# Attention, SoLU block and routed experts on one core: scatters declared independent, a fourth buffer for low parts, and both halves of a product in one slot

## Chip, cores and metric

The kernel runs on one core of one Trainium2 chip. The metric is the device time of one execution in microseconds, lower is better. Matmul operands are `float32r`: each value is kept as a high part and a low part, and a product is three matmuls (high by high, high by low, low by high).

## What is computed

Three layers in a row, over 8 batches of 3072 rows (24576 rows of 256 values):

```python
scores = (1/S) * z @ z.T                       # z: 8 x 3072 x 64
x = u * (relu(scores)**2 @ v)                  # attention, 256 columns
h = x @ w_in; sm = softmax(h); solu = h * sm   # 1024 columns
x = layernorm(solu) * g_ln @ w_out             # back to 256
logits = x @ w_gate; e = argmax(logits)        # 8 experts
out[row] = gate * (relu(x @ w1[e]) @ w2[e])    # w1: 256x1024, w2: 1024x256
```

## The kernel before

**Slots.** The whole program is one list of slots, written out by hand. Slot `n` of the attention is one block of 128 keys against a chunk of 512 queries: 8 batches of 6 chunks of 24 blocks are `NS` = 1152 slots. In a slot TensorE makes the scores `s` of a block four slots ahead (2 matmuls; blocks that were kept from the transposed pair are read back from memory instead) and adds the block at hand to the output, `pe_av`: 6 matmuls `o` of 128x512. ScalarE makes `r` (relu), `a` (square) and the high part `ah`; VectorE subtracts to get the low part `al` (`dve_lo`, line 463). `al` has three buffers, and in slot `n` it is made for block `n+2`.

**The block after the attention.** Each chunk's result is gated, split (`split_x`, line 492) and then worked on in the slots of the next chunk, four groups of 128 rows, one group every six slots: `blk_h` (line 503) is the first product, 12 matmuls `h`, of which the half `kd=0` is issued in slot `w` and the half `kd=1` in slot `w+1`; then maximum, exponent, a transposition over memory (`pb`, `moved`, `pT`), the split `pth`/`ptl`, and `blk_y` (line 577), 24 matmuls `yp` in two halves in two neighbouring slots. `blk_scale`, `blk_logits` and `blk_route` then compute the expert and the place of each row, with many small steps that go back and forth between GpSimd and VectorE (`vv`, `yi`, `rs`, `lg`, `gm`, `gk`, `gs`, `oh`, `ps`, `pf`, `pi`). `blk_scatter` (line 684) writes the 128 rows of a group to their places in `sorted_rows` in memory, by an indirect transfer that GpSimd issues.

**The experts.** `NU` = 62 units follow, 41 of 512 rows and 21 of 256, each with one expert's weights. A table of the first 37 (`n_early`) is made when chunks up to the fifth from the end have been counted, so that the units can start while the last chunks are still being routed; the table of the rest is made at the end. A unit has 8 steps. A step is `up` (6 matmuls `g`, relu on ScalarE, line 899, low part on VectorE, line 900) and, two steps later, `down` (12 matmuls `y`). The product `g` has two banks. After a unit's last `down`, each half of `y` is copied and its rows are written to their places in `out_y` by two indirect transfers from GpSimd (line 931), issued right there in the program.

**Loads.** For units from the third on, the rows `x` (8 pieces and the row numbers `gi`, `load_x`, line 830) and the weights (`load_w`, line 845, 1 MB each for `w1` and `w2`) are issued by SyncE, in order: rows 14 steps before the unit, `w1` of unit `i+2` in step 3 of unit `i` and `w2` in step 6. The split of those weights (`split_w`, lines 854 and 855) stands in steps 0 to 2 and 2 to 5 of unit `i+1`. Once the counts are final, `pad_tail` (line 771) writes 256 rows of padding behind each expert's rows, one expert every two steps from slot `NS+92` on, in SyncE's queue too: one transfer of 128x2x264.

**What waits.** The framework orders all transfers that touch the same tensor in memory by its own analysis: a scatter into `sorted_rows` or `out_y` waits until the one before has landed, a load of rows from `sorted_rows` waits for the scatters issued before it, a scatter for the loads before it, and a piece of padding for the piece before it.

Of the kernel before, what the change touches and what calls it, by code (L numbers as in the profile page):

```python
# [10 lines left out]
F32 = mybir.dt.float32  # L11
# [22 lines left out]
def attention_moe_kernel(ctx, tc, u, v, z, w_in, w_out, g_ln, w_gate, w1, w2, out):  # L34
# [56 lines left out]
    pad_row = const.tile([P, RW], F32, name="pad_row")  # L91
# [4 lines left out]
    index = const.tile([1, n_most], F32, name="index")  # L96

# [12 lines left out]
    with tc.manual_schedule():  # L110
# [14 lines left out]
        V.memset(pad_row[:, D:D + 1], PAD_ID)  # L125
# [3 lines left out]
    with ExitStack() as st:  # L129
# [111 lines left out]

        def fill_dummy():
            for h in range(HALF // P):
                nc.sync.dma_start(out=xs[DUMMY + h * P:DUMMY + (h + 1) * P], in_=pad_row)
# [255 lines left out]
        h_t, p_t, pt_t, y_t, st_t = {}, {}, {}, {}, {}  # L500
        pb_t, pT_t = {}, {}
# [133 lines left out]
        def blk_route(c, part):  # L635
# [23 lines left out]
            elif part == 5:  # L659
# [5 lines left out]
                G.tensor_tensor(out=counts, in0=cum[:, 3], in1=oh[:, 3], op=ALU.add)  # L665
                V.reciprocal(out=s["gs"], in_=s["gs"])
# [28 lines left out]
        def unit_table(parts, tail):  # L695
# [20 lines left out]
            for lo, n, size in parts:  # L716
# [5 lines left out]
                if size == HALF:  # L722
# [14 lines left out]
                ge = tb.tile([1, NE, n_most], F32, tag="ge", name="ge")[:, :, :n]  # L737
                it = index[:, :n]
                V.tensor_scalar(out=rw_f, in0=it, scalar1=float(size), scalar2=first, op0=ALU.mult, op1=ALU.add)
                yield  # L740
                V.tensor_tensor(out=ge, in0=it.unsqueeze(1).to_broadcast([1, NE, n]),
                                in1=pre.unsqueeze(2).to_broadcast([1, NE, n]), op=ALU.is_ge)
                yield
                V.tensor_reduce(out=ex_f, in_=ge.rearrange("o e n -> o n e"), axis=AX.X, op=ALU.add)
                yield
                V.tensor_tensor(out=ge, in0=ge, in1=step.unsqueeze(2).to_broadcast([1, NE, n]), op=ALU.mult)
                yield
                V.tensor_reduce(out=more_f, in_=ge.rearrange("o e n -> o n e"), axis=AX.X, op=ALU.add)
                V.tensor_tensor(out=rw_f, in0=rw_f, in1=more_f, op=ALU.add)
                yield  # L750
# [13 lines left out]
        table = {}  # L764

        def table_step(key, *args):
            if key not in table:
                table[key] = unit_table(*args)
            next(table[key], None)
# [21 lines left out]
        def take(name):  # L791
# [20 lines left out]
            elif name == "set1":  # L812
# [7 lines left out]
                c += [own(ap, "al", [P, CH], bufs=3) for _ in range(3)]  # L820
# [9 lines left out]
        def load_x(i, part=None):  # L830
# [10 lines left out]
            todo.append((gi_t[i][:, :n // P], unit[:, D:D + 1].rearrange("(q p) w -> p (q w)", p=P)))  # L841
            for dst, x in todo if part is None else todo[3 * part:3 * part + 3]:
                dma_of(i).dma_start(out=dst, in_=x)
# [66 lines left out]
        def down(k):  # L910
# [11 lines left out]
            for h, y in enumerate(y_p.pop(i)):  # L922
# [6 lines left out]
                for r in range(2):  # L929
                    q = 2 * h + r  # L930
                    G.indirect_dma_start(
                        out=out, out_offset=bass.IndirectOffsetOnAxis(ap=id_t[i][:, q:q + 1].bitcast(U32), axis=0),
# [209 lines left out]
```

## Time and profile before

| | us |
|---|---|
| median of three runs | 4299.98 |
| lowest and highest | 4298.31, 4304.7 |
| the profiled execution, its own time | 4297.59 |
| its span, first to last instruction | 4296.0 |
| TensorE busy in the span | 4218.8 (98%) |
| VectorE, ScalarE, GpSimd busy | 3173.4, 2773.7, 1368.9 |
| granted TensorE clock, mean | 0.994 of full |

A line of groups gives an operation's line, its shape and count, its busy time with the mean of one in ns, and the idle time just before it with what ended it. A line of waits gives who waited for whom, the total, how often and the longest. Matmuls overlap: one of 128x512 is drawn about 0.39 us long, and the next begins about 0.23 us after it, so the distance of two starts tells the pace, and a busy share of 100% does not tell that the pace is the best one.

### The profile page before, as it was taken

Reading aid. Unit: us, or ns where it says so; the run is one execution under the profiler, and the core shown is the slowest. Engines: PE = TensorE matmul, PEld = TensorE weight load, DVE = VectorE, ACT = ScalarE, POOL = GpSimd, SP = SyncE. Lnnn points to the kernel's source line nnn. Section 1 sums busy time; section 2 is a strip of 40 time slices with the busy share of each in tenths; the row PEclk is TensorE's granted clock in tenths of the full one; section 3 lists DMA queues with packets and bytes.
Section 4 is the critical chain, followed back from the end, with each engine's and each line's share of the span. In section 5 each row is a group of like instructions: output and inputs, shape, how many; then the busy total and the mean of one; then the engine's idle time right before and its main releaser. Section 6 shows DMA issues by size and latency. Waiting matters only on the chain.

```text
span 4296.0 us, 74103 instructions
## 1 busy us (share of the span) xinstructions
PE 4218.8 (98%) x23314; PEld 3659.4 (85%) x23314; DVE 3173.4 (74%) x5485; ACT 2773.7 (65%) x5104; POOL 1368.9 (32%) x2852
## 2 busy tenths in 40 slices
PE   7999999999999999999999999999889999999998
PEld 5888888888888888888888888888788899999998
DVE  8778787777878777787877778777655555555686
ACT  7767776776777677667767766775544444444565
POOL 5135224323522432352244235224322111111111
PEclk9999999999999999999999999999999999999999
DMA  6898789789888988997898898789655555555585
GB/s 160 168 173 180 171 181 176 165 183 174 179 170 182 175 166 183 173 177 171 182 174 168 183 174 176 169 169 181 143 143 132 147 147 134 145 137 147 156 221 162
DMA packets 2444332, 719.11 MB, mean 167 GB/s; under 512 B 2251933, under 2 KB 2325917, under 8 KB 2443936
## 3 DMA queue, kind: packets, MB, share of 16 engines
q1 hardware_dynamic: 2402016, 603.29, 69.2%
q0 software_dynamic: 40864, 110.95, 8.7%
q8 instruction: 182, 2.98, 0.3%
q14 instruction: 214, 1.75, 0.1%
q10 hardware_dynamic: 1056, 0.13, 0.0%
HBM read 442.35 MB, written 273.49 MB: 167 GB/s over the span
## 4 chain that ended last, share of the span: by engine, by line
PE 81%; issue 5%; DMA 4%; DVE 2%; SPq 2%; POOL 1%; ACT 1%; POOLq 0%; DVEq 0%; ACTq 0%
PE o L105 11%; PE o L106 11%; PE o L107 11%; PE yp L105 4%; PE yp L107 4%; PE yp L106 4%; PE h L512 4%; PE h L513 4%; PE h L516 4%; PE s L444 3%; PE s L445 3%; PE y L107 3%; PE y L106 3%; PE y L105 3%; PE g L105 3%
## 5 line engine op out<-in xcount | busy, mean ns | idle before, releaser
L106 PE MATMUL o<-al,vw 128*128 128x512 f32 x2304 | 908.2, 394 | 7.8 <-DVE al L465 7.3
L105 PE MATMUL o<-ah,vw 128*128 128x512 f32 x2304 | 907.8, 394 | 1.7 <-DVE ut L489 1.7
L107 PE MATMUL o<-ah,vw 128*128 128x512 f32 x2304 | 898.7, 390 | 0.0
L450 ACT ACTIVATE r<-s 128x512 f32<-128x512 f32 x704 | 416.7, 592 | 405.6 <-PE s L445 397.1
L460 ACT ACTIVATE ah<-a 128x512 fp32r<-128x512 f32 x832 | 525.3, 631 | 201.6 <-issue 99.5
L465 DVE TENSOR_TENSOR al<-a,ah 128x512 fp32r<-128x512 f32 x832 | 581.4, 699 | 15.7 <-ACT ah L460 14.7
L107 PEld LDWEIGHTS o<-ah,vw 128*128 128x128 f32 x2304 | 433.7, 188 | 94.4
L106 PEld LDWEIGHTS o<-al,vw 128*128 128x128 f32 x2304 | 433.6, 188 | 94.2 <-DVE al L465 16.3
L105 PEld LDWEIGHTS o<-ah,vw 128*128 128x128 f32 x2304 | 433.6, 188 | 84.9 <-ACT ah L460 2.1
L455 ACT ACTIVATE a<-r 128x512 f32<-128x512 f32 x704 | 438.0, 622 | 58.2 <-DVE al L465 29.5
L899 ACT ACTIVATE zw_x<-g 128x512 fp32r<-128x512 f32 (+1 forms) x332 | 179.9, 542 | 428.9 <-PE g L107 425.2
L107 PE MATMUL yp<-gw,ptl 128*128 128x264 f32 x1536 | 437.8, 285 | 7.0 <-DVE ptl L102 7.0
L105 PE MATMUL yp<-gw,pth 128*128 128x264 f32 x1536 | 438.8, 286 | 1.1 <-ACT pth L101 1.1
L106 PE MATMUL yp<-gw,pth 128*128 128x264 f32 x1536 | 438.0, 285 | 0.0
L900 DVE SCALAR_TENSOR_TENSOR zw_x<-g,zw_x 128x512 fp32r<-128x512 f32 (+1 forms) x332 | 205.6, 619 | 308.8 <-ACT zw_x L899 308.7
L102 DVE TENSOR_TENSOR ptl<-pT,pth 128x512 fp32r<-128x512 f32 x384 | 264.2, 688 | 215.8 <-ACT pth L101 213.7
L686 POOL DMA_INDIRECT sorted_rows<-y,pi x192 | 211.7, 1102 | 390.3 <-DMA sorted_rows<-y,pi 307.9
L513 PE MATMUL h<-w_in,xt 128*128 128x512 f32 x768 | 304.9, 397 | 0.0
L512 PE MATMUL h<-w_in,xt 128*128 128x512 f32 x768 | 304.6, 397 | 0.0
L105 PEld LDWEIGHTS yp<-gw,pth 128*128 128x128 f32 x1536 | 289.2, 188 | 16.9 <-ACT pth L101 1.5
L106 PEld LDWEIGHTS yp<-gw,pth 128*128 128x128 f32 x1536 | 289.9, 189 | 15.0
L107 PEld LDWEIGHTS yp<-gw,ptl 128*128 128x128 f32 x1536 | 290.1, 189 | 7.7 <-DVE ptl L102 7.7
(271 smaller groups left out, 10665.7 us busy)
## 6 DMA issues: line engine op xcount, KB each, us to landing
vw_x<-in_moe_w SPq DMA_DIRECT2D x120, 1024.0 KB
pT<-moved SPq DMA_DIRECT2D x768, 128.0 KB
sym<-kept SPq DMA_DIRECT2D x1520, 64.0 KB
kept<-sym SPq DMA_DIRECT2D x316, 256.0 KB
moved<-pb SPq DMA_DIRECT2D x528, 128.0 KB
moved<-pb POOLq DMA_DIRECT2D x240, 128.0 KB, 3.1
x<-sorted_rows SPq DMA_DIRECT2D x312, 64.0 KB
sym<-kept SPq DMA_DIRECT2D x68, 256.0 KB
```

The lines of the kernel that those rows point to most:

```text
L102: V.tensor_tensor(out=lo, in0=src, in1=hi.bitcast(F32), op=ALU.subtract)
L105: T.matmul(out=out, lhsT=lh, rhs=rh, start=start, stop=False, **kw)
L106: T.matmul(out=out, lhsT=lh, rhs=rl, start=False, stop=False, **kw)
L107: T.matmul(out=out, lhsT=ll, rhs=rh, start=False, stop=stop, **kw)
L450: A.activation(out=r, in_=s_t.pop(n), func=AF.Relu)
L455: A.activation(out=a, in_=r_t.pop(n), func=AF.Square)
L460: A.activation(out=h, in_=a_t[n], func=AF.Copy)
L465: V.tensor_tensor(out=l, in0=a_t[n], in1=ah_t[n].bitcast(F32), op=ALU.subtract)
L512: T.matmul(out=h[:, fs], lhsT=w[:, 0, kd, ts_], rhs=w_in_t[0][:, kd, fs], start=(kd == 0), stop=False)
L513: T.matmul(out=h[:, fs], lhsT=w[:, 0, kd, ts_], rhs=w_in_t[1][:, kd, fs], start=False, stop=False)
L686: G.indirect_dma_start(out=xs[:DUMMY], out_offset=bass.IndirectOffsetOnAxis(ap=pi[:, t:t + 1].bitcast(U32), axis=0), in_=y_t[c][:, t, :], ...
L900: V.scalar_tensor_tensor(out=lo, in0=h, scalar=0.0, in1=hi.bitcast(F32), op0=ALU.max, op1=ALU.subtract)
```

## The change

Six things, in the order of the diff:

- The row of padding in SBUF shrinks from 264 to 72 values, and `pad` writes the padding of 256 rows with three transfers (one for the last 8 columns, two for 256 columns in pieces of 64) where there was one.
- `al` gets a fourth buffer, and `dve_lo` is issued for block `n+3` instead of `n+2`, in the slot in which its high part is made.
- Scatters into `sorted_rows` are declared independent of each other, and those of rows that came after the early table ("late rows") of the loads of the early units ("early units"), in both directions. Before each indirect transfer GpSimd clears one value, `gap`.
- The arrays of the unit tables are worked on in two halves of four experts.
- Scatters into `out_y` are declared independent of each other, and issued one or two steps later in the program, ahead of that step's `up`; those of the last unit stay where they were.
- For 46 of the 48 chunks, `blk_h` with `kd=0` and `blk_y` with `h=0` move one slot later, into the slot of their other half; `split_x` of a chunk moves to the first slot of the next one.

```diff
+        def pad(rows):
+            nh, nz = HALF // P, D // 64
+            nc.sync.dma_start(out=rows[:, D:].rearrange("(h p) w -> p h w", p=P),
+                              in_=pad_row[:, 64:].unsqueeze(1).to_broadcast([P, nh, RW - D]))
+            for h in range(nh):
+                nc.sync.dma_start(out=rows[h * P:(h + 1) * P, :D].rearrange("p (k c) -> p k c", k=nz),
+                                  in_=pad_row[:, :64].unsqueeze(1).to_broadcast([P, nz, 64]))
...
-            l = ap.tile([P, CH], F32R, tag="al", name="al", bufs=3)
+            l = ap.tile([P, CH], F32R, tag="al", name="al", bufs=4)
...
+        def between():
+            G.memset(gap, 0.0)
+
+        def apart(i, *groups, why):
+            for g in groups:
+                tc.declare_no_dep(i.ins, group=g, reason=why)
+
         def blk_scatter(c, t):
             pi = st_t[c]["pi"]
-            G.indirect_dma_start(
+            between()
+            i = G.indirect_dma_start(
...
+            apart(i, "rows", "late rows", why="every token has a row of its own")
+            apart(i, "early units", why="units of the early table are full of rows counted before")
+            tc.add_to_no_dep_group("late rows" if table and c not in counted else "rows", i.ins)
...
-            nc.sync.dma_start(out=xs[ds(r, HALF)].rearrange("(h p) w -> p h w", p=P),
-                              in_=pad_row.unsqueeze(1).to_broadcast([P, HALF // P, RW]))
+            pad(xs[ds(r, HALF)])
...
             for dst, x in todo if part is None else todo[3 * part:3 * part + 3]:
-                dma_of(i).dma_start(out=dst, in_=x)
+                d = dma_of(i).dma_start(out=dst, in_=x)
+                if i < n_early:
+                    apart(d, "late rows", why="units of the early table are full of rows counted before")
+                    tc.add_to_no_dep_group("early units", d.ins)
...
                 for r in range(2):
-                    q = 2 * h + r
-                    G.indirect_dma_start(
...
+                    if i == NU - 1:
+                        send(i, 2 * h + r, o[:, r * D:(r + 1) * D])
+                    else:
+                        sends[k + 1 + h].append((i, 2 * h + r, o[:, r * D:(r + 1) * D]))
+
+        sends = defaultdict(list)
+
+        def send(i, q, o):
+            between()
+            d = G.indirect_dma_start(
...
+            apart(d, "out", why="every token has a row of its own")
+            tc.add_to_no_dep_group("out", d.ins)
...
-                at(w, blk_h, c, t, 0)
+                whole = c < NCHUNK - 2
+                at(w + whole, blk_h, c, t, 0)
                 at(w + 1, blk_h, c, t, 1)
...
-                at(y, blk_y, c, t, 0)
+                at(y + whole, blk_y, c, t, 0)
                 at(y + 1, blk_y, c, t, 1)
...
+                for args in sends.pop(k - LAG, []):
+                    send(*args)
                 if 0 <= k < NP:
                     up(k)
...
-                    dve_lo(i - 2)
                     put(i - 2)
                     a_t.pop(i - 2)
+                if 0 <= i - 1 < NS:
+                    dve_lo(i - 1)
...
-                if 0 <= n < NS and n % NKB == NKB - 1:
+                if 0 <= n < NS and n % NKB == NKB - 1 and n // NKB >= NCHUNK - 2:
                     split_x(n // NKB)
+                if 0 < n < NS and n % NKB == 0 and n // NKB < NCHUNK - 1:
+                    split_x(n // NKB - 1)
```

**Three places in the order of the instructions.** In brackets stand the semaphores that an instruction waits for: `DMASW` are those of GpSimd's transfers and `DMAHW` those of SyncE's, eight of each, used in turn; the name of an engine is that of its work.

GpSimd before, while a unit's rows are sent out and the last but one chunk is routed (`lg`, `gm`, `gs` are steps of the routing, `a_x` the copied half of `y`):

```order
L625 TENSOR_TENSOR lg<-y,rs 128x32 [waits Pool_49]
L931 DMA out_y<-a_x,ids 24576x256 [waits DMASW1_49,DVE_49]
L931 DMA out_y<-a_x,ids 24576x256 [waits DMASW2_49]
L931 DMA out_y<-a_x,ids 24576x256 [waits DMASW3_49,Activation_49]
L931 DMA out_y<-a_x,ids 24576x256 [waits DMASW5_49,DMASW4_49]
L642 TENSOR_TENSOR lg<-lg,gm 128x32 [waits Pool_49]
L658 TENSOR_SCALAR gs<-gs 128x4 [waits DVE_49]
```

And now, at the same step of the routing:

```order
L634 TENSOR_TENSOR lg<-y,rs 128x32 [waits Pool_49]
L695 MEMSET gap 1x1
L966 DMA out_y<-a_x,ids 24576x256 [waits DMASW2_49,DVE_49]
L695 MEMSET gap 1x1 [waits Pool_49]
L966 DMA out_y<-a_x,ids 24576x256 [waits DMASW3_49]
L651 TENSOR_TENSOR lg<-lg,gm 128x32
L695 MEMSET gap 1x1 [waits Pool_49]
L966 DMA out_y<-a_x,ids 24576x256 [waits DMASW4_49,Activation_49]
L695 MEMSET gap 1x1 [waits Pool_49]
L966 DMA out_y<-a_x,ids 24576x256 [waits DMASW5_49]
L667 TENSOR_SCALAR gs<-gs 128x4 [waits DVE_49]
```

The second and the fourth transfer waited for the one just before; each now waits for the one that used its semaphore eight transfers ago, and the routing step `lg<-lg,gm` stands between the two pairs and not behind all four.

SyncE's queue before, at the first two paddings, behind the load of the next `w1` (`vw_x<-in_moe_w`):

```order
L849 DMA vw_x<-in_moe_w 128x2x1024 [waits DMAHW6_49,DVE_49]
L773 TENSOR_LOAD tail_i [waits DVE_49]
L773 ISA x2
L774 ISA
L774 DMA sorted_rows<-pad_row 128x2x264 [waits DMAHW4_49,DMAHW3_49,DMAHW5_49,DMAHW2_49,DMAHW7_49,DMAHW1_49,DMAHW0_49]
L773 TENSOR_LOAD tail_i
L773 ISA x2
L774 ISA
L774 DMA sorted_rows<-pad_row 128x2x264 [waits DMAHW7_49]
L846 TENSOR_LOAD expert_i
```

And now:

```order
L876 DMA vw_x<-in_moe_w 128x2x1024 [waits DMAHW7_49,DVE_49]
L796 TENSOR_LOAD tail_i [waits DVE_49]
L796 ISA x2
L245 ISA
L245 DMA sorted_rows<-pad_row 128x2x8 [waits DMAHW0_49,DMAHW1_49,DMASW7_49,DMAHW2_49,DMASW6_49,DMAHW3_49,DMASW5_49,DMAHW4_49,DMASW4_49,DMAHW5_49,DMASW3_49,DMAHW6_49,DMASW2_49,DMASW1_49]
L248 ISA
L248 DMA sorted_rows<-pad_row 128x4x64 [waits DMAHW0_49]
L248 ISA
L248 DMA sorted_rows<-pad_row 128x4x64 [waits DMAHW1_49]
L796 TENSOR_LOAD tail_i
L796 ISA x2
L245 ISA
```

One transfer of 128x2x264 has become three, and the second and third of them wait for the one before, as the next padding does for the third.

TensorE before, at the slot in which one half of a product `h` stands between the scores and `pe_av` (`o`); the other half stands in the slot next to it:

```order
L444 MATMUL s<-zw 128x512
L445 MATMUL s<-zv,zw 128x512
L512 MATMUL h<-w_in_137,xt 128x512
L513 MATMUL h<-w_in_138,xt 128x512
L512 MATMUL h<-w_in_137,xt 128x512
L513 MATMUL h<-w_in_138,xt 128x512
L516 MATMUL h<-w_in_137,xt 128x512 x2
L105 MATMUL o_4620<-ah,vw 128x512
L106 MATMUL o_4620<-al,vw 128x512
L107 MATMUL o_4620<-ah,vw 128x512
L105 MATMUL o_4624<-ah,vw 128x512
L106 MATMUL o_4624<-al,vw 128x512
```

And now:

```order
L452 MATMUL s<-zw 128x512
L453 MATMUL s<-zv,zw 128x512
L521 MATMUL h<-w_in_138,xt 128x512
L522 MATMUL h<-w_in_139,xt 128x512
L521 MATMUL h<-w_in_138,xt 128x512
L522 MATMUL h<-w_in_139,xt 128x512
L525 MATMUL h<-w_in_138,xt 128x512 x2
L521 MATMUL h<-w_in_138,xt 128x512
L522 MATMUL h<-w_in_139,xt 128x512
L521 MATMUL h<-w_in_138,xt 128x512
L522 MATMUL h<-w_in_139,xt 128x512
L525 MATMUL h<-w_in_138,xt 128x512 x2
```

Both halves follow each other, and `pe_av` comes once behind the pair. The halves of `yp` stand in the same way. The count of matmuls is the same.

## Rows read from the trace of the kernel before

**Rows 1.** The page of before: matmuls on `al`, their idle time and its cause.

```profile
L106 PE MATMUL o<-al,vw 128*128 128x512 f32 x2304 | 908.2, 394 | 7.8 <-DVE al L465 7.3
```

**Rows 2.** Busy time by stretch: span, then PE, PEld, DVE, ACT, POOL; then clock.

```profile
0.00:200.00 200.00, 173.37 (x784) 136.95 (x785) 160.64 (x251) 146.65 (x267) 66.47 (x82) 0.98 0.74 165
200.00:2900.00 2700.00, 2699.32 (x13735) 2290.29 (x13735) 2127.87 (x3625) 1935.34 (x3490) 988.00 (x2324) 1.00 0.88 175
2900.00:3400.00 500.00, 463.19 (x2691) 407.80 (x2690) 313.48 (x591) 236.17 (x434) 155.23 (x288) 0.96 0.64 145
3400.00:4200.00 800.00, 800.00 (x5430) 742.46 (x5429) 509.81 (x889) 403.88 (x795) 140.60 (x143) 1.00 0.60 159
```

**Rows 3.** Waits of TensorE, 200 to 2900 us: total, times, longest us.

```profile
PE o L106 <- DVE al L465: 0.5, 1, 0.5
```

**Rows 4.** Waits of TensorE from 2900 to 3420 us.

```profile
PE g L105 <- DVE zw_x L900: 26.3, 7, 7.1
PE yp L107 <- DVE ptl L102: 7.0, 3, 6.6
```

**Rows 5.** Waits of VectorE from 2900 to 3420 us.

```profile
DVE yi L608 <- POOL vv L604: 24.6, 3, 9.1
...
DVE gk L648 <- POOL lg L642: 12.5, 1, 12.5
```

**Rows 6.** Timeline of GpSimd: start us, us, operation [idle before <- ended by].

```profile
3132.89 0.98 POOL L931 DMA_INDIRECT out_y<-a_x,ids  x1 [3.22 <-DMA out_y<-a_x,ids]
3133.88 0.26 POOL L642 TENSOR_TENSOR lg<-lg,gm 128x32 f32<-128x32 f32 x1
```

**Rows 7.** Timeline of TensorE around the longest of these stalls.

```profile
3137.35 0.80 PE L105 MATMUL g<-vw_x 128*128 128x512 f32 x1 [7.09 <-DVE zw_x L900]
3137.94 0.63 PE L106 MATMUL g<-vw_x 128*128 128x512 f32 x1
```

**Rows 8.** Timeline of SyncE's queue, 3379 to 3404 us: issue us, us, transfer, count.

```profile
3379.84 0.40 SPq L849 DMA_DIRECT2D vw_x<-in_moe_w  x1
3381.56 4.93 SPq L774 DMA_DIRECT2D sorted_rows<-pad_row  x2
3387.27 0.40 SPq L849 DMA_DIRECT2D vw_x<-in_moe_w  x1
3388.45 5.76 SPq L774 DMA_DIRECT2D sorted_rows<-pad_row  x2
3397.39 4.25 SPq L843 DMA_DIRECT2D x<-sorted_rows  x8
...
3403.08 0.40 SPq L849 DMA_DIRECT2D vw_x<-in_moe_w  x1
```

**Rows 9.** Waits of SyncE's queue from 3340 to 3430 us.

```profile
SPq L843 <- DMA sorted_rows<-y,pi: 37.5, 3, 17.5
SPq L774 <- DMA sorted_rows<-pad_row: 15.9, 4, 4.5
SPq L843 <- DMA sorted_rows<-pad_row: 3.5, 2, 2.4
```

**Rows 10.** Timeline of ScalarE at the first of the two late weight loads.

```profile
3357.15 0.63 ACT L854 ACTIVATE vw_x<-vw_x 128x512 fp32r<-128x512 f32 x1 [6.41 <-DMA vw_x<-in_moe_w]
```

**Rows 11.** Timeline of TensorE: two starts of an up product, one step apart.

```profile
3506.92 0.40 PE L105 MATMUL g<-a_x,ur_x 128*128 128x512 f32 x1
...
3509.74 0.40 PE L105 MATMUL g<-a_x,ur_x 128*128 128x512 f32 x1
```

**Rows 12.** Timeline of TensorE: six `o` after half `h`, six after `s`.

```profile
1003.80 0.39 PE L105 MATMUL o<-ah,vw 128*128 128x512 f32 x1
...
1005.19 0.39 PE L444 MATMUL s<-zw 128*128 128x512 f32 x1
...
1016.38 0.39 PE L105 MATMUL o<-ah,vw 128*128 128x512 f32 x1
...
1017.74 0.40 PE L512 MATMUL h<-w_in,xt 128*128 128x512 f32 x1
```

More of the change, by code (lines that the diff above doesn't have):

```diff
@@ L90, in attention_moe_kernel @@
     counts = const.tile([P, NE], BF16, name="counts")
-    pad_row = const.tile([P, RW], F32, name="pad_row")
+    pad_row = const.tile([P, 64 + RW - D], F32, name="pad_row")
     expert_i = const.tile([1, NU], I32, name="expert_i")
@@ L96, in attention_moe_kernel @@
     index = const.tile([1, n_most], F32, name="index")
+    gap = const.tile([1, 1], F32, name="gap")
     V, A, G, T = nc.vector, nc.scalar, nc.gpsimd, nc.tensor
@@ L124, in attention_moe_kernel @@
         V.memset(pad_row, 0.0)
-        V.memset(pad_row[:, D:D + 1], PAD_ID)
+        V.memset(pad_row[:, 64:65], PAD_ID)
         V.memset(n_used, 0.0)
@@ L240, in load_consts @@
             nc.sync.dma_start(out=g_sb, in_=g_ln.rearrange("(k p) -> p k", p=P))
+        def pad(rows):
[5 more added lines that the diff above has]
+                                  in_=pad_row[:, :64].unsqueeze(1).to_broadcast([P, nz, 64]))
         def fill_dummy():
-            for h in range(HALF // P):
-                nc.sync.dma_start(out=xs[DUMMY + h * P:DUMMY + (h + 1) * P], in_=pad_row)
+            pad(xs[DUMMY:])
         def step_w(b):
@@ L500, in attention_moe_kernel @@
         h_t, p_t, pt_t, y_t, st_t = {}, {}, {}, {}, {}
+        table, routed, counted = {}, [], []
         pb_t, pT_t = {}, {}
@@ L665, in blk_route @@
                 G.tensor_tensor(out=counts, in0=cum[:, 3], in1=oh[:, 3], op=ALU.add)
+                routed.append(c)
                 V.reciprocal(out=s["gs"], in_=s["gs"])
@@ L736, in unit_table @@
                 ex_f, rw_f, more_f = [t1(k, n_most)[:, :n] for k in ("ex_f", "rw_f", "more_f")]
-                ge = tb.tile([1, NE, n_most], F32, tag="ge", name="ge")[:, :, :n]
+                ge = tb.tile([1, NE // 2, n_most], F32, tag="ge", name="ge")[:, :, :n]
                 it = index[:, :n]
                 V.tensor_scalar(out=rw_f, in0=it, scalar1=float(size), scalar2=first, op0=ALU.mult, op1=ALU.add)
+                V.memset(ex_f, 0.0)
                 yield
[L741 to L750, printed above, removed]
+                for es in (slice(0, NE // 2), slice(NE // 2, NE)):
+                    each = [x[:, es].unsqueeze(2).to_broadcast([1, NE // 2, n]) for x in (pre, step)]
+                    for x, y in ((ex_f, None), (rw_f, each[1])):
+                        if y is None:
+                            V.tensor_tensor(out=ge, in0=it.unsqueeze(1).to_broadcast([1, NE // 2, n]), in1=each[0],
+                                            op=ALU.is_ge)
+                        else:
+                            V.tensor_tensor(out=ge, in0=ge, in1=y, op=ALU.mult)
+                        V.tensor_reduce(out=more_f, in_=ge.rearrange("o e n -> o n e"), axis=AX.X, op=ALU.add)
+                        V.tensor_tensor(out=x, in0=x, in1=more_f, op=ALU.add)
+                        yield
                 V.tensor_scalar(out=ex_f, in0=ex_f, scalar1=float(NE - 1), scalar2=None, op0=ALU.min)
@@ L762, in unit_table @@
                 yield
-        table = {}
         def table_step(key, *args):
@@ L768, in table_step @@
                 table[key] = unit_table(*args)
+                if key == 0:
+                    counted.extend(routed)
             next(table[key], None)
@@ L819, in take @@
                 c += [own(ap, "ah", [P, CH], bufs=4) for _ in range(4)]
-                c += [own(ap, "al", [P, CH], bufs=3) for _ in range(3)]
+                c += [own(ap, "al", [P, CH], bufs=4) for _ in range(3)]
                 for i, k in enumerate(("w1h", "w1l", "w2h", "w2l")):
```

7 lines of the change are left out of this document (5 added, 2 removed).

## Prediction

> **What bounds the kernel now.** I read the busy time by stretch first, because a share over the whole span hides where TensorE rests. From 200 to 2900 us it is busy for 2699.32 of 2700 us, and from 3400 to 4200 us for all of 800 [rows 2]: there only its own pace counts. It rests in the first 200 us, where the loads and the preparation of the weights run, and from 2900 to 3400 us, where the first expert units run while the last chunks are still routed: 463.19 of 500 us, 36.8 us of rest, at a granted clock of 0.96 [rows 2]. So the change can win in that stretch, or in the pace of the matmuls, and hardly anywhere else.
>
> What ends the rests of that stretch is read from the waits. TensorE waits 26.3 us in seven stalls for the low part of the up product, and 7.0 us for `ptl` [rows 4], both VectorE's work. VectorE itself stood waiting for GpSimd's small routing steps: 24.6 us in three waits for `vv`, 12.5 us in one for `lg` [rows 5]. And GpSimd stood in its own queue: the fourth scatter into `out_y` began 3.22 us after the queue was free, ended by the scatter before it, and `lg` came right behind it [rows 6]. A routing step of 0.26 us thus waits for a copy and four scatters in a row, VectorE for it, and TensorE for VectorE. Two of the seven stalls have another chain: SyncE waited 37.5 us in three waits to load rows, because scatters of the last chunk into the same tensor were still to come [rows 9], the weights queued behind those rows came late, and ScalarE stood 6.41 us for them [rows 10].
>
> After such a stall TensorE also runs at half speed: the matmul after the 7.09 us stall begins the next one 0.59 us later and that one is drawn 0.63 us long, where an undisturbed one is drawn 0.40 [rows 7, 11]. About six such matmuls follow each stall, some 0.2 us each and 0.3 more for the first: 1.5 us, and for eight stalls 12 us.
>
> **Scatters.** The order of GpSimd shows both remedies: no scatter waits for the one before, and the routing step stands between pairs whose copies were made a step earlier. The added `gap` costs GpSimd one small operation per scatter, like the 0.26 us of [rows 6]; GpSimd is busy 155 of 500 us [rows 2], so it is covered, and without that cover would cost 1 us a unit. The rows of the early units no longer wait for the last scatters, which takes away the other chain too. Gain: 26.3 + 7.0 + 12 = 45 us. The ends are 33, if only the rests go and the clock falls anyway, and 36.8 + 12 = 49, if every rest of the stretch goes.
>
> **Both halves in one slot.** TensorE's matmuls are the same. But the pace depends on the neighbour: six `o` right after half an `h` take 1005.19 - 1003.80 = 1.39 us, after scores 1017.74 - 1016.38 = 1.36 [rows 12]. With the halves together that slow passage comes once per product where it came twice. There are 184 groups with two such products each, 368 x 0.03 = 11 us at most; the starts are rounded to 0.01, so one passage is 0.02 to 0.04, and behind `yp` I have no such pair of rows. I take 7, between 0 and 11, nearer to what the row shows.
>
> The Trainium skill, page "TensorE: Matmul & The Clock Gate", section "Back-to-back issue gap", gives an isolated gap of N/2.4 + 2.5 ns, which for 512 columns is 215.8 ns whatever stands before. By that, six `o` would take 1.295 us in both places and the halves would gain nothing, which makes the sum 7 us longer; the rows show neither the value nor the indifference.
>
> **Low parts a slot earlier, four buffers.** TensorE waited for `al` for 7.3 us in the whole run [rows 1], of which 0.5 us from 200 us on [rows 3]. The rest lies at the start, where VectorE is busy 160.64 of 200 us [rows 2]: making `al` sooner there makes something else later. I take 2, between 0 and 7. The moved `split_x`, the tables in halves and the memory saved cost nothing on the path: VectorE is busy 313 of 500 us in the stretch where the tables are made [rows 2]; without that cover the few dozen small operations would be some us.
>
> **Padding: the price.** Three transfers instead of one, each waiting for the one before, all in the queue that also loads the weights. Now one unit with four paddings takes that queue 3403.08 - 3379.84 = 23.24 us from one `w1` to the next [rows 8], against 8 steps of 3509.74 - 3506.92 = 2.82 us [rows 11], 22.6 us: it just fits. The change adds eight waits per unit. The paddings that stand behind a 1 MB load waited 15.9 us in four waits, those read by a row load 3.5 us in two [rows 9]. The added ones stand behind other paddings, so I take the second kind, 1.75 us, and get 23.24 + 14 = 37.2 us per unit, over two units 74.4 us. That `w1` lands some 4.5 us later, as long as the padding behind such a load waited at longest [rows 9], and is wanted 21 steps, 59.2 us, after the first; ScalarE may be late by about a step, 2.8 us, since the up product has two banks. So the delay is 74.4 + 4.5 - 59.2 - 2.8 = 17 us, as two or three new stalls of ScalarE on the weights, clock included. With the shorter wait (3.5 - 2.4 = 1.1 us) it is 7 us, with the mean of all six (19.4 / 6 = 3.2) it is 40.
>
> **Sum.** 4297.6 - 45 - 7 - 2 + 17 = 4260.6 us on the profiled execution. The median of three runs is 2.4 us above it, so 4263.
>
> **Rivals.**
> - *The paddings are absorbed.* The row loads are issued 14 steps ahead and SyncE now reaches the paddings on time. For it: half of its time was waiting. Against: the queue has 22.6 us and needs 37. Time: 4263 - 17 = 4246.
> - *The short pieces land slowly,* as slowly as the mean of the six waits, 3.2 us: 40 instead of 17, so 4286. For it: the pieces are 64 values and 8 values long, where a whole row of 264 was written; against: they carry no more bytes together. Beside it stands the Trainium skill, page "DMA: Bandwidth & Descriptors", section "Specifications": below 512 bytes a transfer does a read-modify-write. No row before shows such a write to this tensor.
> - *The change does not free GpSimd.* What ends most of its waits may be the copies and not the scatters. Then half of the 45 us stay: 4285. The order speaks against it: the sends stand a step behind their copies.
> - *Slower: the bunched halves starve TensorE.* A slot with a whole product becomes long, and the two beside it short, the 1.36 us of six `o` [rows 12] and the scores, in which ScalarE must do a relu, a square and a high part. VectorE, now issuing `al` in the slot of its high part, stands for ScalarE. If TensorE waits 0.1 us behind each of 368 products the whole gain is gone; at 0.3 us it is 110 us, 4263 + 110 = 4373. Against: from 200 to 2900 us TensorE waited once, 0.5 us [rows 3], and ScalarE is busy 72% and VectorE 79% of that time [rows 2].
>
> **How the numbers follow.** Forecast 0.50, absorbed 0.20, slow pieces 0.14, not freed 0.08, starved 0.08. Runs of this kernel tell 0.2%, 8.6 us, from no change. Faster: the first two, and three quarters of the next two, 0.86; within 0.2%: 0.07; slower: 0.07, most of the last. The forecast's own range is 4250 to 4280, by the bounds of the paddings and of the halves. The range reaches from 4238, where the paddings are absorbed and the upper ends of 49 and 11 come true, to 4287.
>
> **What would show it.** From 2900 to 3360 us TensorE busy nearly throughout, no wait of VectorE for `vv`, `lg` or `ps` above 2 us, no wait of SyncE for a scatter; `o` behind `h` slow once per group; then, some 30 to 80 us behind the first padding, ScalarE waiting 5 to 11 us for weights two or three times, with SyncE's waits for paddings near 24 x 1.75 us. It is wrong if TensorE shows waits for `r`, `ah` or `al` between 200 and 2900 us, if the stalls on the routing stay, or if the paddings leave TensorE busy or cost over 30 us.

## The result, and the profile after the change

Median of six runs 4262.45 us (4258.74 to 4263.86) against 4301.94 us (4298.15 to 4304.7) for the kernel before in the same series: ratio 0.9908, 95% interval 0.9895 to 0.9921. The forecast was 4263, its range 4238 to 4287. The profiled execution took 4262.3 us, its span is 4260.7.

Read in the order of the prediction, first the busy time by stretch: span, then PE, PEld, DVE, ACT, POOL, then the granted clock (behind it stand the DMA engines' share and GB/s).

```profile
0.00:200.00 200.00, 169.71 (x754) 135.65 (x755) 155.21 (x247) 143.30 (x261) 60.51 (x68) 0.97 0.69 160
200.00:2900.00 2700.00, 2700.00 (x13802) 2297.39 (x13801) 2147.79 (x3640) 1929.90 (x3510) 1040.44 (x2513) 1.00 0.83 176
2900.00:3400.00 500.00, 481.00 (x2884) 427.42 (x2883) 332.88 (x643) 243.93 (x449) 167.83 (x367) 0.98 0.66 156
3400.00:4200.00 800.00, 799.21 (x5474) 743.92 (x5474) 516.19 (x906) 410.92 (x822) 162.68 (x288) 1.00 0.61 159
```

Against [rows 2] there are three changes. From 2900 to 3400 us TensorE rests 19.0 us where it rested 36.8. From 200 to 2900 us it is as busy as before, but does 13802 matmuls where it did 13735: 67 more, the pace. And in the first 200 us it rests 3.7 us more, which the prediction did not have.

What ends TensorE's rests from 2900 to 3420 us (total, times, longest), beside [rows 4]:

```profile
PE g L106 <- DVE zw_x L927: 9.4, 3, 5.4
PE g L106 <- DVE zv_x L927: 7.5, 1, 7.5
PE o L106 <- DVE ut L497: 1.7, 1, 1.7
```

The tiles are like those of before, but the cause is another. GpSimd's timeline, at a routing step between two pairs of sends, beside [rows 6]:

```profile
3093.85 1.00 POOL L966 DMA_INDIRECT out_y<-a_x,ids  x1 [0.21 <-issue]
3094.86 0.27 POOL L651 TENSOR_TENSOR lg<-lg,gm 128x32 f32<-128x32 f32 x1
3095.05 0.09 POOL L695 MEMSET gap<- 1x1 f32 x1
3095.33 0.98 POOL L966 DMA_INDIRECT out_y<-a_x,ids  x1 [0.19 <-issue]
```

No scatter stands for the one before: 0.2 us lie between them where 3.22 lay. GpSimd still stands for the copies that it sends, longer than before even: from 2900 to 3420 us 217.0 us in 14 waits, where it was 127.9 in 13. But VectorE has no wait for `vv`, `lg` or `ps` of over 2 us any more. What it waits for there is ScalarE (25.6 us in four waits for the split of the weights), and ScalarE for weights; its timeline has three long waits of this kind in a row, beside [rows 10]:

```profile
3357.72 0.63 ACT L881 ACTIVATE vw_x<-vw_x 128x512 fp32r<-128x512 f32 x1 [8.43 <-DMA vw_x<-in_moe_w]
...
3374.96 0.63 ACT L881 ACTIVATE vw_x<-vw_x 128x512 fp32r<-128x512 f32 x1 [13.60 <-DMA vw_x<-in_moe_w]
...
3396.02 0.63 ACT L881 ACTIVATE zd_x<-vw_x 128x512 fp32r<-128x512 f32 x1 [5.92 <-DMA vw_x<-in_moe_w]
```

The weights are late because SyncE's queue is full of paddings. Its timeline (issue, us, transfer, count) over the first two units with paddings, beside [rows 8], and its waits from 3300 to 3500 us, beside [rows 9]:

```profile
3311.57 0.40 SPq L876 DMA_DIRECT2D vw_x<-in_moe_w  x1
3318.60 0.41 SPq L245 DMA_DIRECT2D sorted_rows<-pad_row  x1
3320.46 2.46 SPq L248 DMA_DIRECT2D sorted_rows<-pad_row  x2
...
3329.47 0.41 SPq L876 DMA_DIRECT2D vw_x<-in_moe_w  x1
3330.73 0.37 SPq L245 DMA_DIRECT2D sorted_rows<-pad_row  x1
3335.22 2.61 SPq L248 DMA_DIRECT2D sorted_rows<-pad_row  x2
...
3352.43 0.40 SPq L876 DMA_DIRECT2D vw_x<-in_moe_w  x1
...
3391.03 1.61 SPq L876 DMA_DIRECT2D vw_x<-in_moe_w  x2
```

```profile
SPq L876 <- DVE vw_x L882: 30.4, 5, 7.6
SPq L248 <- DMA sorted_rows<-pad_row: 24.9, 13, 3.9
...
SPq L245 <- DMA sorted_rows<-pad_row: 5.3, 4, 2.5
SPq L245 <- DMA sorted_rows<-y,pi: 4.8, 1, 4.8
SPq L867 <- DMA sorted_rows<-pad_row: 1.9, 2, 1.0
```

The first line is of weight loads that wait until the split has emptied their buffer. From one `w1` to the next the queue now takes 3352.43 - 3311.57 = 40.9 us, then 3391.03 - 3352.43 = 38.6, where a unit of 512 rows lasts 22.6; in the 40.9 are the 4.8 us for which the first padding stands for a scatter. The row loads (L867) wait for no scatter any more, where they stood 37.5 us. Behind the longest stall TensorE is slow again, as in [rows 7]:

```profile
3376.97 0.80 PE L106 MATMUL g<-a_x,ur_x 128*128 128x512 f32 x1 [7.45 <-DVE zv_x L927]
3377.57 0.63 PE L107 MATMUL g<-vr_x,ur_x 128*128 128x512 f32 x1
3377.99 0.63 PE L108 MATMUL g<-a_x 128*128 128x512 f32 x1
```

And the pace, beside [rows 12]: six `o` behind a whole `h`, then six behind other `o`.

```profile
1007.62 0.39 PE L106 MATMUL o<-ah,vw 128*128 128x512 f32 x1
...
1009.00 0.39 PE L106 MATMUL o<-ah,vw 128*128 128x512 f32 x1
...
1010.36 0.39 PE L452 MATMUL s<-zw 128*128 128x512 f32 x1
```

The passage still costs 1009.00 - 1007.62 = 1.38 us against 1010.36 - 1009.00 = 1.36, but it comes once per product. The second product gains inside itself too. Its 24 matmuls in a row, to the first `o` behind them, and then the two twelves of the kernel before:

```profile
1012.17 0.29 PE L106 MATMUL yp<-gw,pth 128*128 128x264 f32 x1
...
1015.08 0.40 PE L106 MATMUL o<-ah,vw 128*128 128x512 f32 x1
```

```profile
1010.24 0.29 PE L105 MATMUL yp<-gw,pth 128*128 128x264 f32 x1
...
1011.70 0.39 PE L105 MATMUL o<-ah,vw 128*128 128x512 f32 x1
...
1013.09 0.29 PE L105 MATMUL yp<-gw,pth 128*128 128x264 f32 x1
...
1014.56 0.39 PE L105 MATMUL o<-ah,vw 128*128 128x512 f32 x1
```

They take 2.91 us where they took 1.46 + 1.47 = 2.93.

### The profile page after: what moved, and what is told of

It is laid out like the page before. It is cut to its first block, busy times and chain, and to the rows that moved or that the text cites. A ratio compares the mean times of both kernels' runs of the same rounds, so it can differ in the third digit from the quotient of the medians.

```text
span 4260.7 us, 74414 instructions
## 1 busy us (share of the span) xinstructions
PE 4198.9 (99%) x23314; PEld 3653.1 (86%) x23314; DVE 3187.5 (75%) x5509; ACT 2755.7 (65%) x5104; POOL 1443.4 (34%) x3254
## 4 chain that ended last, share of the span: by engine, by line
PE 92%; issue 3%; DMA 2%; DVE 1%; POOL 1%; ACT 1%; SPq 1%; POOLq 0%; DVEq 0%; ACTq 0%
PE o L106 12%; PE o L107 12%; PE o L108 12%; PE yp L107 4%; PE yp L106 4%; PE yp L108 4%; PE h L521 4%; PE h L525 4%; PE h L522 4%; PE y L108 4%; PE y L107 4%; PE y L106 4%; PE s L452 4%; PE s L453 4%; PE g L106 3%; PE g L107 3%
## 5 line engine op out<-in xcount | busy, mean ns | idle before, releaser
L452 PE MATMUL s<-zw 128*128 128x512 f32 x704 | 277.7, 394 | 22.1 <-ACT r L458 15.3
L537 DVE TENSOR_REDUCE nm<-h 128x1 f32<-128x1024 f32 x192 | 234.6, 1222 | 72.8 <-PE h L525 64.2
```

The costliest lines, as they stand in the source:

```text
L452: T.matmul(out=s, lhsT=w, rhs=z_t[c], start=True, stop=False)
L537: V.tensor_reduce(out=s["nm"][:, t:t + 1], in_=h, axis=AX.X, op=ALU.max, negate=True)
```

## The experiments

Times are medians, of four or five runs each; the kernel before stood between 4299.4 and 4303.2 in these series. Differences are taken to the changed kernel's 4262.45, measured in a series of its own; with the kernel before 3.8 us apart from series to series, a difference of under 4 us is not told from none.

**1. Paddings independent of each other.** Between two of them stands a second load of the same register.

```diff
+            def alone(d):
+                if e is not None:
+                    tc.declare_no_dep(d.ins, group="pads", reason="every padding has rows of its own")
+                    tc.add_to_no_dep_group("pads", d.ins)
```

> The changed kernel with the paddings declared independent of each other (a second load of the same register stands between two of them, so that they need not follow one another); what is still waited for is the transfer eight places earlier in the queue, and the row loads before. Theory (the serial waits of the paddings hold back the weights of the next units): SyncE's waits between paddings go, ScalarE's two waits of 13.6 and 8.4 us for weights fall to at most one short one, and the time falls from 4262.5 by 12 to 22 us, to 4240-4250. Rival (it is not their waits on each other but the transfers themselves that land slowly, as short pieces would): the row loads behind them wait as long as before in place of the paddings, and the time stays within 4259-4264.

Measured 4241.09 us (ratio to before 0.9854, 0.9839 to 0.9869), 21.4 us less. The stretch from 3300 to 3450 us, of the changed kernel and then of this one (columns as above):

```profile
3300.00:3450.00 150.00, 134.09 (x812) 120.52 (x811) 83.14 (x188) 58.13 (x107) 26.43 (x49) 0.93 0.53 133
```

```profile
3300.00:3450.00 150.00, 149.90 (x959) 135.93 (x959) 97.43 (x211) 68.83 (x127) 29.94 (x55) 1.00 0.63 154
```

15.8 us of rest go, and the granted clock is 1.00 where it was 0.93; the other 5.6 us fit the slow matmuls behind three stalls. The pieces are the same, so it was their waits and not their length.

**2. Each padding in one transfer, the waits kept.** The room for the wide row comes from the tables, made in quarters.

```diff
-    pad_row = const.tile([P, 64 + RW - D], F32, name="pad_row")
+    pad_row = const.tile([P, RW], F32, name="pad_row")
...
+            nc.sync.dma_start(out=rows.rearrange("(h p) w -> p h w", p=P),
+                              in_=pad_row.unsqueeze(1).to_broadcast([P, HALF // P, RW]))
```

> The changed kernel with each padding in one transfer of whole rows again, each still waiting for the one before; the room for the wide row comes from making the table in quarters instead of halves. Theory (a padding costs by the number of serial waits): 16 of 24 waits go and nearly all of the 21 us that independent paddings gave, 4240-4248, with SyncE's waits for paddings near those of before, 15 to 20 us in all. Rival (the row loads now come earlier, so that even single transfers, each waiting, hold back the weights): half of the loss stays, 4250-4258.

Measured 4241.04 us (0.9863, 0.9848 to 0.9878): the same 21.4 us. From 3300 to 3450 us TensorE is busy 149.90 us here too. So one transfer per padding costs nothing even if each waits, and three that don't wait cost nothing either; only three that wait do. The memory for the fourth buffer of `al` could thus have come from the tables alone.

**3. The halves in two slots again.**

```diff
-                whole = c < NCHUNK - 2
+                whole = False
```

> The changed kernel with the two halves of each feed-forward product in two slots again; everything else as changed. Theory (each slow passage from half a product to the next matmul costs some 0.02 to 0.04 us, and the change halves their number): slower by 7 to 11 us, 4269-4274, spread evenly over 200 to 2900 us as fewer matmuls in the same time, with no wait of TensorE there. Rival (the better pace of that stretch comes from the low part made a slot sooner or from the moved split of the gated input): within 2 us of 4262.5.

Measured 4272.96 us (0.9933, 0.992 to 0.9947), 10.5 us more; 13756 matmuls from 200 to 2900 us where the changed kernel does 13802, and no wait of TensorE there. The theory holds at its upper end, though only in part by the passages to `o` from which it was worked out. Where the gain lies can be read from the distances of consecutive starts in both traces, from 300 to 2800 us. The mean for `yp` is 122.2 ns in this run and 121.1 in the changed kernel, for `o` 229.6 and 228.7, for `h` 233.7 and 233.5. Over the 184 groups that gives an estimate of 4.8 us in `yp` itself and 5.8 in `o`.

**4. The low part two slots behind its scores again.** Four buffers stay.

```diff
                 if 0 <= i - 2 < NS:
+                    dve_lo(i - 2)
...
-                if 0 <= i - 1 < NS:
-                    dve_lo(i - 1)
```

> The changed kernel with the low part made two slots behind the scores again, as before; its four buffers stay. Theory (in the first 200 us VectorE is the busy engine, and the low part made sooner there pushes the square roots and copies of the start back): TensorE is busy 173 of the first 200 us again where it was 169.7, the wait for the low part returns to 5 to 8 us, and the time falls by 2 to 4 us, to 4258-4261. First rival (the lost 4 us at the start come from something else): the time stays within 1.5 us of 4262.5 and TensorE busy near 169.7. Second rival (the earlier low part is what keeps the pace from 200 to 2900 us): slower by up to 9 us, 4265-4272.

Measured 4279.31 us (0.9947, 0.9934 to 0.9961): 16.9 us more, twice what the second rival gave it. The waits of TensorE from 200 to 2900 us now hold what the changed kernel hasn't at all:

```profile
PE o L107 <- DVE al L473: 10.6, 14, 0.9
```

**5. Both undone.** Edits 3 and 4 together.

> The changed kernel with both undone, the halves in two slots and the low part made two slots behind its scores. Alone, the first cost 10.5 us and the second 16.9 us. Theory (the earlier low part only matters where the halves stand together: it keeps TensorE from waiting in the long slot, and without bunching there is nothing to wait for): about as the halves alone, 4271-4277, and no wait of TensorE for the low part above 1 us in all from 200 to 2900 us. Rival (each has its own worth): the sum of both, 4287-4292.

Measured 4275.8 us (0.9943, 0.993 to 0.9957), a time as the theory has it, and no wait for the low part. But from 200 to 2900 us TensorE has a wait that neither the kernel before nor the changed one has:

```profile
PE h L521 <- ACT xt L102: 3.8, 7, 0.7
```

`xt` is the high part of the chunk that `split_x` splits, and it is late once per batch. The move of `split_x` to the next chunk stays in this edit, so this run is not the order of before; that the move makes the wait was not tried by itself. The four corners:

| | low part a slot later | low part as changed |
|---|---|---|
| halves in two slots | 4275.8 | 4273.0 |
| halves in one slot | 4279.3 | 4262.45 |

With the late low part the halves in one slot win nothing (3.5 us slower, which is not told from none), with the early one 10.5. The early low part alone gives 2.8 us, not told from none either and no more than the waits for `xt` that go with it; together with the halves it gives 16.9. The start: TensorE is busy 171.8 of the first 200 us with both undone, 170.8 with the late low part alone, 168.8 to 170.2 in the runs with the early one, so 1 to 2 us of the 3.7 lost there hang on it. TensorE's waits in these 200 us, before and then as changed, say how:

```profile
PE s L444 <- ACT r L450: 9.5, 7, 3.9
PE o L106 <- DVE al L465: 6.8, 8, 1.9
```

```profile
PE s L452 <- ACT r L458: 15.3, 7, 4.0
...
PE o L107 <- DVE al L473: 2.5, 3, 1.4
```

What TensorE no longer waits for `al` it waits for `r`; in experiment 4 the wait for `r` is at 9.2 us again, and that for `al` at 9.3. Where the rest of the loss comes from was not tried by itself.

**6. The waits of the scatters put back,** for the early row loads too. The outputs are still sent later.

```diff
-            for g in groups:
-                tc.declare_no_dep(i.ins, group=g, reason=why)
+            pass
```

> The changed kernel with every scatter and every early row load waiting again for the scatters before it; the later sending of the outputs stays. Theory (the waits in GpSimd's queue made the stalls on the routing): the stalls of 3 to 7 us in front of the up product return between 2900 and 3400 us and the time rises by 30 to 45 us, to 4292-4308. Rival (it is enough that the outputs are sent a step later, between which the routing step can run): at most 12 us slower, 4263-4275, and no wait of VectorE for a routing step above 5 us.

Measured 4284.66 us (0.9965, 0.9951 to 0.9978), 22.2 us more: between the two expectations.

**7. Early row loads and late scatters wait for each other again;** scatters among themselves don't.

```diff
-                if i < n_early:
+                if False:
                     apart(d, "late rows", why="units of the early table are full of rows counted before")
```

> The changed kernel with the row loads of the early units waiting for the last chunks' scatters again; the scatters still don't wait for each other. Theory (these loads stand ahead of the weights in SyncE's queue, so the weights come later again): slower by 5 to 12 us, 4267-4275, with waits of SyncE for scatters near 10 us and the loss between 3300 and 3450 us. Rival (with the scatters free of each other the last of them is done before the row load is due): within 2 us of 4262.5.

Measured 4275.89 us (0.9944, 0.9931 to 0.9958), 13.4 us more: above the theory's 12, and over half of what the waits of experiment 6 cost. SyncE's waits from 3300 to 3500 us:

```profile
SPq L867 <- DMA sorted_rows<-y,pi: 30.7, 2, 16.0
```

The loss is not where it was expected: TensorE's rest from 2900 to 3300 us grows from 3.1 to 8.3 us, that from 3300 to 3450 us only from 15.9 to 19.7. The first is one new stall, and its chain is another: the edit makes scatters wait for row loads too, and the first rows are loaded by GpSimd itself, in the queue of its scatters and routing steps. GpSimd's timeline, and TensorE's at the stall:

```profile
2995.85 1.38 POOL L867 DMA_DIRECT2D x<-sorted_rows  x2 [5.35 <-issue]
...
3001.41 1.03 POOL L704 DMA_INDIRECT sorted_rows<-y,pi  x1 [3.33 <-DMA gi<-sorted_rows]
```

```profile
3004.89 0.59 PE L108 MATMUL yp<-gw,ptl 128*128 128x264 f32 x1 [5.23 <-DVE ptl L103]
```

Behind the scatter comes the routing step `vv`. VectorE stands 6.58 us for it, and makes `ptl` right behind.

**8. Each output sent right behind its copy.** No scatter waits.

```diff
-                    if i == NU - 1:
+                    if True:
                         send(i, 2 * h + r, o[:, r * D:(r + 1) * D])
```

> The changed kernel with each output scatter issued right behind the copy it sends, as before; no scatter waits for another. In the run with the waits put back (4284.7 us) the later sending stayed, and 22 us of some 47 us that the stretch from 2900 to 3400 us had gained came back. Theory (the other part is the order: GpSimd stands in its queue for the copy, and routing steps behind it stand too): slower by 10 to 25 us, 4272-4288, with waits of VectorE for routing steps of 3 us and more between 2900 and 3300 us. Rival (it is enough that scatters don't wait for each other): within 4 us of 4262.5.

Measured 4262.41 us (0.9914, 0.9901 to 0.9928): no difference. The rival is right: without waits the place of the sends is worth nothing.

**9. Both, waits put back and outputs sent at once.**

> The changed kernel with both parts of the work on the scatters undone: scatters and early row loads wait again, and each output scatter stands right behind its copy. The waits alone cost 22.2 us, the place of the sends alone nothing. Theory (the two stand in for each other: a later send hides part of what the waits cost): 40 to 50 us slower than the changed kernel, 4302-4312, with waits of VectorE for routing steps of 5 us and more, as before the change. Rival (the parts add up, and the rest of the gain came from elsewhere): 4282-4288, like the waits alone.

Measured 4320.15 us (1.0046, 1.0032 to 1.0059), 57.7 us more, above the theory's range and slower than the kernel before. VectorE's waits from 2900 to 3450 us are those of [rows 5] again:

```profile
DVE yi L617 <- POOL vv L613: 17.1, 2, 8.9
...
DVE gk L657 <- POOL lg L651: 12.7, 1, 12.7
```

So the later send is worth 35.5 us (57.7 - 22.2) while the scatters wait, and nothing once they don't. By the terms that are left of the change, 4302.4 + 21.4 for the paddings - 9.7 for halves and low parts (against the kernel before, see experiment 10), this should have been about 4314; the 6 us above stay open, in a run whose executions lie 13 us apart.

**10. The work on the scatters with nothing else of weight:** edits 2, 3 and 4 together.

> The work on the scatters with nothing else of weight: the changed kernel with the halves in two slots, the low part two slots late, and each padding in one transfer. If the terms add up as the runs so far have them (13.3 us for the first two together, 21.4 us for the paddings), this is 4262.5 + 13.3 - 21.4 = 4254 us, and the scatters are worth 48 us against the kernel before. Rival (the delay by the paddings hides part of what the pace gains, or the other way round): more than 4 us off that, below 4250 or above 4258.

Measured 4254.17 us (0.9889, 0.9873 to 0.9904), on the forecast to 0.2 us where its runs are 3.4 us apart, and 48.2 us below the 4302.36 of before in its series. The terms add up. They are terms between these runs, though: this one, too, keeps the moved `split_x` and waits 3.8 us for `xt`. Its matmuls come in the same order as those of the kernel before, so the two traces can be laid on each other. At the 1385th matmul of the scores, which starts at 2933.8 us before, it is 5.3 us behind; from 3400 us on it is 43.2 ahead. The stretch in between gained 48.5 us. The changed kernel starts the same matmul 9.7 us earlier than before: so much, and not 13.3, are its halves, its low parts and the moved `split_x` worth against the kernel before, by these two traces.

**11. The second product beside a first one,** on top of edit 2, to see how far the bunching carries.

```diff
-                out_, back, cut_, y = (4, 6, 11, 13) if last else (5, 8, 12, 15) if c < NCHUNK - 3 else (5, 7, 10, 12)
+                out_, back, cut_, y = (4, 6, 11, 13) if last else (5, 8, 14, 18) if c < NCHUNK - 3 else (5, 7, 10, 12)
```

> One transfer per padding (4241.0 us), and in all but the last three chunks the second feed-forward product is made three slots later, in the slot in which the first product of a later block stands, right ahead of it. Theory (what counts is how often TensorE passes from such a product to the attention's matmuls; this takes away 180 of 368 passages of 0.02 to 0.03 us): 3 to 6 us faster, 4235-4238. Rival (the slot becomes long and five short ones follow, in which ScalarE and VectorE don't keep up): TensorE waits for the high or low part by 0.1 us and more in each of some 180 groups, 4250-4300.

Measured 4533.31 us (1.0544, 1.0527 to 1.0562). TensorE's and SyncE's greatest wait from 200 to 2900 us:

```profile
PE o L106 <- DVE ut L493: 100.7, 34, 4.5
```

```profile
SPq L571 <- DVE ptl L103: 533.5, 128, 10.8
```

The edit does a second thing: it makes the split of a transposed block later, but not the load of the next one into the same buffer, so SyncE stands for the split and every load behind it comes late.

**12. The same with that load two slots later** (`(5, 10, 14, 18)`), and with edit 8.

> One transfer per padding and the outputs sent right behind their copies (each cost nothing against 4241 us); and the second product beside a first one again, in which TensorE lost 292 us before. There the split of the transposed block had been made two slots later and its load not: SyncE stood 533.5 us in 128 waits for the split, and the loads of kept blocks behind it came late. Now that load is two slots later too. Theory (SyncE's queue was the cause, the crowded slot is not): the waits of SyncE for the split fall to some 60 us as before, those of ScalarE for kept blocks to 20 us, and the fewer passages give 3 to 6 us, 4235-4238. Rival (one slot of 7 us and five short ones are too uneven for ScalarE and VectorE): TensorE still waits from 200 to 2900 us for high and low parts or the gate, and the time is above 4246.

Measured 4427.57 us (1.0294, 1.028 to 1.0308): the later load gives back 106 of 292 us, and 187 stay. TensorE waits for the gated chunk (`ut`) at the turn from chunk to chunk, and VectorE stands for the first product, which now lies behind the second in the slot (65.5 us in 85 waits in experiment 2):

```profile
PE o L106 <- DVE ut L493: 80.6, 34, 2.5
```

```profile
DVE nm L533 <- PE h L521: 324.4, 150, 2.3
```

SyncE's wait for the split fell to 244.8 us, not to the 60 of the theory, so how much of the 187 us is still the queue and how much the crowded slot stays open; that VectorE's stand at `nm` makes its gating late was not tried by itself. What is shown is that bunching one step further, in this form, starves TensorE.

Kernels 1 and 2, at 4241 us, are the fastest: about 21 us below the changed kernel, 1.4% below the one before.

## Why the prediction came out right

The measured terms, by experiments 10, 5 and 2, make the result: 4302.4 - 48.2 - 13.3 + 21.4 = 4262.3 us. The mechanisms of the two largest terms were right; that 4263 is met within 0.6 us is luck. The kernel before stood 2.4 us higher in that series than in the three runs of the forecast, the scatters gave 3.2 us more than forecast, halves and low parts 4.3 more, and the paddings took 4.4 more: these nearly cancel.

- **Scatters, forecast 45 us, measured 48.2.** The size holds, within its ends of 33 and 49; by the traces of experiment 10 and of before the stretch itself gained 48.5 and 5.3 were lost ahead of it (the two profiled executions are 45.8 us apart, the medians 48.2). Of the 48.5, 33.1 are rest that went (36.8 to 3.7 us from 2900 to 3450), as the 33.3 forecast; the 15.4 that remain stand against the 12 for slow matmuls behind the stalls. The prediction spoke of two remedies, no waits and sends a step later. They stand in for each other: with the waits gone the later sending is worth nothing (experiment 8), with the waits there 35.5 us (9 less 6). And of the 22.2 us of the waits with the later sending in place, 13.4 come by row loads and scatters that wait for each other (7): in part by SyncE's loads, the chain to which the prediction gave two of seven stalls, in part by a scatter behind GpSimd's own row load, which it did not have. The added `gap`, 0.09 us each, was covered as forecast.
- **Halves, forecast 7 us, measured 10.5,** between its ends of 0 and 11. The price of one passage to `o` was well taken: 0.02 stood there, and the rows of after give 0.02 again. What was short is the second product, for which the prediction said that it had no rows: nearly half of the gain lies inside `yp` (experiment 3). That experiment shows that the pace depends on how the matmuls are bunched, and six `o` take 1.36 us at best, 227 ns each. Against it stood the Trainium skill, page "TensorE: Matmul & The Clock Gate", section "Back-to-back issue gap": its formula for an isolated matmul, N/2.4 + 2.5 ns, gives an estimate of 215.8 ns for 512 columns and has no term for what stands before, so it gave nothing for the halves. The runs agree with neither the value nor the indifference.
- **Low parts, forecast 2 us: the mechanism was wrong.** The prediction looked for the gain at the start; there is none, since TensorE's waits for `al` turn into waits for `r`. The 2.8 us of the low part alone are within the spread, and no more than waits for `xt` that the kernel before does not have. Its worth is that it makes the gain of the halves possible: without it TensorE waits 10.6 us for `al` and the halves win nothing instead of 10.5. That the pair comes near the 7 + 2 of the sum, 9.7 us by the traces of before and after, is luck. This is the starving rival, with VectorE's `al` in the place of ScalarE's work; the prediction did not see that another part of the change took it away. The row that it held against that rival, one wait of TensorE from 200 to 2900 us, came from the even order and could say little of the uneven one.
- **Paddings, forecast 17 us, measured 21.4** (1 and 2). The mechanism is as told: a queue that takes 38.6 to 40.9 us per unit (37.2 forecast) where 22.6 are to be had, then three waits of ScalarE for weights. The waits of the second kind were well chosen: in the second unit the eight added ones cost (38.6 - 23.24) / 8 = 1.9 us each, against 1.75. What was short is the queue's time over the two units, 3391.03 - 3311.57 = 79.5 us where 74.4 stood, and 4.8 of these 5.1 are the first padding's wait for a scatter, which was to be gone. The weights then landed 5.0 us behind their issue, where 4.5 stood: with the measured values the sum gives 79.5 + 5.0 - 59.2 - 2.8 = 22.5 us.
- **The other rivals.** Absorbed paddings would have been 4246; the stalls of 8.43 and 13.60 us exclude it. Pieces that land slowly would have been 4286; their waits were 1.9 us on the mean (24.9 in 13) and not 3.2, and the same pieces without waits (1) give the time of whole rows (2), 4241.09 and 4241.04. Beside it stood the Trainium skill, page "DMA: Bandwidth & Descriptors", section "Specifications", with its read-modify-write below 512 bytes; if it acts here, it shows in no time, since TensorE does not rest for the paddings in either run. Of the rival that GpSimd is not freed the premise holds, most of its waits are ended by the copies; its conclusion does not, since the routing steps no longer come late for VectorE.
- **Not forecast:** the 3.7 us lost in the first 200 us. They are within the measured terms: 173.37 - 171.80 = 1.6 in that of experiment 10 (TensorE's busy time there), which keeps the moved `split_x`, the other 2.1 in that of halves and low parts.

Of what the profile was to show, all came but three things: one wait of SyncE for a scatter is left, 4.8 us at the first padding; ScalarE's longest wait was 13.60 where up to 11 was told; and SyncE's waits of paddings for paddings were 24.9 + 5.3 = 30.2 us in 17, where 24 x 1.75 = 42 were told.

## What to carry to other kernels

Before you split one transfer into several to save memory, count the waits this adds in the queue, and compare the queue's time per unit with the unit's; if the pieces touch different rows, declare them independent. Two remedies for one stall need not add: undo each alone and both together before you keep both. If an order bunches one engine's work, look whether its suppliers have to come earlier, and try both with and without; here the bunching gave nothing alone. And when you undo parts one by one, read the trace of each run for waits that neither end has: a part that stayed can spoil the count.

## What the runs showed of the hardware

TensorE's pace depends on how matmuls are bunched: six of 512 columns took 1.36 us behind their like, 1.38 to 1.39 behind another product, and 264 columns took 122.2 ns each in twelves and 121.1 in a row of 24, at a granted clock of 1.00; bunching gave 10.5 us in 4262. After a rest of 7.45 us the granted clock was 0.50 from 3377.0 to 3379.7 us, the lower of the two levels, 1.2 GHz, and from 3383 to 3385 us it was 1.00 again:

```profile
3377.00:3379.70 2.70, 2.70 (x6) 2.12 (x7) 2.70 (x4) 0.60 (x2) 0.00 (x0) 0.50 0.22 54
```

The first matmul behind the rest began the next 0.60 us later and that one the third 0.42 later, where 0.23 is usual. And the paddings in pieces of 64 values that had to wait for the one before them in the same queue stood 1.9 us on the mean (24.9 us in 13 waits, at most 3.9).
